# A linear-attention and feed-forward kernel on one core: q and k projected with 64 rows, two heads at once in the array's halves

## The chip, the core and the metric

The kernel runs on one core of one Trainium2 chip. A core has five engines that work side by side and meet through semaphores: TensorE (matmuls; PE in the profile, its weight loads PEld), VectorE (DVE), ScalarE (ACT), GpSimd (POOL) and SyncE (SP), which here issues nearly all the transfers between the chip's memory and the core's. Matmuls read the on-chip memory SBUF and write PSUM, which has eight banks of 512 float32 numbers on each of 128 partitions. The metric is the device time of one execution in microseconds (us).

## The reference, cut to what matters

Eight batches and eight heads, 576 tokens each, a head dimension of 64 and 128 random features; then a feed-forward block over all 4608 tokens, 512 wide with 2048 inside.

```python
def phi(x):                                    # x is q or k, times 64 ** -0.25
    proj = np.einsum('bhsd,md->bhsm', x, omega)
    sq = np.sum(x * x, axis=-1, keepdims=True) / 2.0
    h = proj - sq
    h = h - np.max(h, axis=-1, keepdims=True)
    return np.exp(h) / np.sqrt(m)
q_p, k_p = phi(q_s), phi(k_s)
kv = np.einsum('bhsm,bhsd->bhmd', k_p, v)
z = np.sum(k_p, axis=2)
num = np.einsum('bhsm,bhmd->bhsd', q_p, kv)
den = np.einsum('bhsm,bhm->bhs', q_p, z)[..., None] + 1e-06
x = num / den                                  # then, over all heads of a token:
h = x @ w_in
sp = np.maximum(h, 0.0) + np.log1p(np.exp(-np.abs(h)))
out = (h * erf(sp)) @ w_out
```

The same number sq is taken from all 128 features of a token, and then the largest feature is taken off.

## The kernel before

**Work items.** Attention goes by pairs of heads: 8 batches of 4 pairs, 32 pairs with 1152 tokens (9 chunks of 128) each. The feed-forward block goes by batch, in two halves of the 2048 inner features; its matmuls have 288 moving columns and run on operands that are split into a high and a low part (tiles xh and xl, gh and gl, and weights w with both), three matmuls for each product. Its first products are h (and hS and hA, in a form with seven products instead of eight from the fourth batch on), its second ones o.

**A pair's attention.** `load` brings q and k, transposed: 64 dimensions on the partitions, 1152 tokens along them (tiles uq and uk, into rows 0 to 63 for q and 64 to 127 for k), and v. A `square` step writes the squares of these numbers into the other 64 rows of the same tile, on GpSimd in two pieces or on ScalarE in one. `project` then runs, per chunk of 128 tokens, one float32 matmul with all 128 rows: the chunk is the stationary operand, and the moving one (wq or wk) holds the scaled omega in the rows of the numbers and the constant -0.5/8 in the rows of the squares, so that the matmul gives proj - sq at once. Three chunks share a PSUM bank (ppq or ppk), and a projection uses three banks, one after the other. VectorE takes the negated maximum of the bank's three chunks (mxq or mxk), and ScalarE the exponentials with it as the bias (fq or fk). Each bank goes through these three steps for itself. Then `key_values` multiplies fk with v (kvp), `turn` transposes fq (pt, copied to qh and ql), and `attend` forms numerator and denominator (nd), which ScalarE and VectorE divide into xs, the feed-forward block's input.

**Weights.** They come as float64 bits (st) and are rebuilt in wt by a step on GpSimd or ScalarE and three on VectorE, split into w by steps on ScalarE, GpSimd or VectorE, and stored (wdw); later uses fetch the split form.

**What sets the order.** `build` names all operations with their operands, costs and due times, and `Plan.order` places them with a list scheduler: each engine takes, among the operations that are ready and for which buffers are free, the one that is due first. The table COST gives TensorE's costs, SLOTS the number of buffers of each kind, and CAPS how many PSUM banks each stream may hold (4 for attention, 5 in the first batch). An operation may have several engines to choose from. The result is a fixed order on each engine; at run time an engine waits where an operand or a buffer isn't ready. The first batch's four pairs run ahead of all feed-forward work; from then on the pairs of the next batch lie between the matmuls of the current one. Transfers of weights are planned up to 40 us before their use.

Every instruction is recorded through one helper, so the profile shows line 742 for nearly all of them (748 in the changed file); they are told apart by their tiles. A float32 matmul of the program shows as two MATMUL records in the profile.

Of the kernel before, what the change touches and what calls it, by code (L numbers as in the profile page):

```python
# [19 lines left out]
P = 128  # L20
B, H, S, D = 8, 8, 576, 64
NP = H // 2
S2 = 2 * S
NC = S2 // P
MID = NC // 2
D1 = D + 1
DM, DF = 512, 2048
T = 288
# [32 lines left out]
SLOTS = dict(w=8, u=3, f=2, mx=3, v=2, qh=1, ql=1, kh=1, kl=1, rc=2, xs=4, xh=2, xl=2, u2=2,  # L61
             hs=4, gs=2, gh=6, gl=6, os=4, ps=8)
CAPS = dict(st=2, wt=2, cv=2, att=4, moe1=3, moe2=2)

# [250 lines left out]
SQN = 4  # L315
SQG = -1e9
SQA = 4.0
# [4 lines left out]
def build(emit):  # L322

    pl = Plan()
# [113 lines left out]
    def early(n):  # L438
        return 5 if n < NP else None

    def load(n, qk):
        a = pairs[n]

        u = a["u" + qk] = pl.tile("hs", f"u{qk}{a['nm']}", [P, S2], F32, "u0") if 0 < n < NP else \
            pl.tile("u", f"u{qk}{a['nm']}", [P, S2])
        parts = 3 if n == 0 else 1
        for i in range(parts):
            keys = [("x", c) for c in range(3)] if parts == 1 else [("x", i)]
            pl.op("load" + qk, [("S", 0.1, 1e9)], lambda e, i=i: E.x_load(u, qk, a, i, parts),
                  writes=[(u, k) for k in keys], size=D * S2 * 4 // parts)  # L450
# [4 lines left out]
        for i in range(parts):  # L455
            keys = range(3) if parts == 1 else [i]
            f = 1.0 / parts
            pl.op("sq" + qk, [("A", 1.17 * f + .1, -1e9)] if n == 0 else
                  [("G", 2.2, SQG if n < SQN else -1e9), ("A", 1.2, -1e9 if n < SQN else SQA)],
                  lambda e, i=i: E.square(e, u, qk, i, parts),  # L460
                  reads=[(u, ("x", c)) for c in keys], writes=[(u, ("s", c)) for c in keys])

    def project(n, qk, t0):
        a = pairs[n]
        u = a["u" + qk]
        f = a["f" + qk] = pl.tile("gs", f"f{qk}{a['nm']}", [P, NC, P], F32, "f0") \
            if 0 < n < NP and qk == "q" else pl.tile("f", f"f{qk}{a['nm']}", [P, NC, P])
        mx = pl.tile("mx", f"mx{qk}{a['nm']}", [P, NC])
        for i in range(3):
            pp = pl.tile("ps", f"pp{qk}{a['nm']}_{i}", [P, 512], F32, "att", early(n))  # L470
            pl.op("proj" + qk, [("T", 3 * COST["proj"], -1e9)], lambda e, i=i, pp=pp: E.project(pp, u, qk, i),
                  reads=[(u, ("x", i)), (u, ("s", i))], writes=[(pp, 0)],
                  plan=pair_time(n, t0 + 0.05 * i))
            pl.op("max" + qk, [("V", 0.56, -1e9)], lambda e, i=i, pp=pp: E.maximum(mx, pp, i),
                  reads=[(pp, 0)], writes=[(mx, i)])
            pl.op("exp" + qk, [("A", 1.1, -1e9)], lambda e, i=i, pp=pp: E.exponential(f, mx, pp, i),
                  reads=[(pp, 0), (mx, i)], writes=[(f, i)], set="exp")

    def key_values(n, t0):
        a = pairs[n]  # L480
        f, v = a["fk"], a["v"]
        kvp = a["kvp"] = pl.tile("ps", "kvp" + a["nm"], [P, 512], F32, "att", early(n))
        for j in range(2):
            pl.op("kv", [("T", (5 - j) * COST["kv"], -1e9)], lambda e, j=j: E.key_values(kvp, f, v, j),
                  reads=[(f, i) for i in range(3)] + [(v, 0)], writes=[(kvp, 0)],
                  plan=pair_time(n, t0 + 0.08 * j))
        whole = n < WHOLE
        kh = a["kh"] = pl.tile("kh", "kh" + a["nm"], [P, 2, P], F32 if whole else F32R)
        kl = a["kl"] = kh if whole else pl.tile("kl", "kl" + a["nm"], [P, 2, P], F32R)
        pl.op("kvhigh", [("V", 0.6, -1e9), ("A", 0.7, -1e9)], lambda e: E.kv_high(e, kh, kvp),  # L490
              reads=[(kvp, 0)], writes=[(kh, 0)])
        if not whole:
            pl.op("kvrest", [("V", 0.6, -1e9)], lambda e: E.kv_rest(kl, kvp, kh),
                  reads=[(kvp, 0), (kh, 0)], writes=[(kl, 0)])

    def turn(n, t0):
        a = pairs[n]
        whole = n < WHOLE
        lent = ("gh", "qh0", 2) if n < NP else ("qh", "qh", None)
        qh = a["qh"] = pl.tile(lent[0], "qh" + a["nm"], [P, S2], F32 if whole else F32R, *lent[1:])  # L500
        ql = a["ql"] = qh if whole else pl.tile("ql", "ql" + a["nm"], [P, S2], F32R)
        for i in range(3):
            pt = pl.tile("ps", f"pt{a['nm']}_{i}", [P, 512], F32, "att", early(n))
            pl.op("turn", [("T", 3 * COST["tr"], -1e9)], lambda e, i=i, pt=pt: E.turn(pt, a["fq"], i),
                  reads=[(a["fq"], i)], writes=[(pt, 0)], plan=pair_time(n, t0 + 0.05 * i))
# [216 lines left out]


@with_exitstack
def tile_attention_moe(ctx: ExitStack, tc: tile.TileContext, qT, kT, vP, omT, w1, w2, out):
# [32 lines left out]
    dve.memset(eps, 1e-6 * P)  # L758

    wq = const.tile([P, P], F32, name="wq")  # L760
    wk = const.tile([P, P], F32, name="wk")
# [5 lines left out]
    half_sq = -0.5 / math.sqrt(D)  # L767
    dve.memset(wk[0:D], half_sq)
    dve.memset(wq[D:P], half_sq)
    dve.tensor_scalar_mul(wk[D:P], om[D:P], scale)  # L770
    dve.tensor_scalar_mul(wq[0:D], om[0:D], scale)

    def copy(e, dst, src):
        if e == "A":
# [9 lines left out]
    def halves(e, n):  # L784

        return (slice(0, n // 2), slice(n // 2, n)) if e == "G" else (slice(0, n),)
# [5 lines left out]
    class Emit:  # L792
# [40 lines left out]
        def fetch(self, dst, src):  # L833
            sp.dma_start(dst, src)

        def x_load(self, u, qk, a, i, parts):
            src = (kT if qk == "k" else qT)[a["b"], a["p"]]
            r = slice(D, P) if qk == "k" else slice(0, D)
            c = slice(i * S2 // parts, (i + 1) * S2 // parts)
            sp.dma_start(u.ap[r, c], src[:, c])  # L840

        def v_load(self, v, a):
            sp.dma_start(v.ap, vP[a["b"], a["p"]])

        def square(self, e, u, qk, i, parts):
            c = slice(i * S2 // parts, (i + 1) * S2 // parts)
            src, dst = (slice(D, P), slice(0, D)) if qk == "k" else (slice(0, D), slice(D, P))
            if e == "G":
                for h in halves(e, S2 // parts):
                    pool.tensor_mul(u.ap[dst, c][:, h], u.ap[src, c][:, h], u.ap[src, c][:, h])  # L850
            else:
                act.activation(u.ap[dst, c], u.ap[src, c], AF.Square)


        def project(self, pp, u, qk, i):
            for c in range(3):
                pe.matmul(pp.ap[:, c * P:(c + 1) * P], lhsT=u.ap[:, (3 * i + c) * P:(3 * i + c + 1) * P],
                          rhs=wq if qk == "q" else wk, start=True, stop=True)

        def maximum(self, mx, pp, i):  # L860
            dve.tensor_reduce(mx.ap[:, 3 * i:3 * i + 3],
                              pp.ap[:, :3 * P].rearrange("p (c m) -> p c m", c=3), axis=AX.X,
                              op=ALU.max, negate=True)

        def exponential(self, f, mx, pp, i):
            for c in range(3):
                act.activation(f.ap[:, 3 * i + c, :], pp.ap[:, c * P:(c + 1) * P], AF.Exp,
                               bias=mx.ap[:, 3 * i + c:3 * i + c + 1])

        def key_values(self, kvp, f, v, j):  # L870

# [164 lines left out]
```

## Time and profile before

| | |
|---|---|
| Time, median of 3 runs | 1103.33 us (1102.34 to 1104.43) |
| Span of the profiled execution | 1101.4 us, on the one core |
| ppk and ppq MATMUL records | 576 each, mean 279 and 275 ns |
| kvp MATMUL records | 576, of which 512 with 65 columns, mean 269 ns |
| o MATMUL records | 3072, mean 298 and 295 ns |
| maxima mxk and mxq on VectorE | 96 each, mean 556 and 557 ns |
| exponentials fk and fq on ScalarE | 288 each, mean 371 ns |
| moved by transfers | 231.27 MB, mean 210 GB/s |

The times are those of unprofiled runs. The span is that of one profiled execution, from its first to its last instruction; a small time around it is not in it. A row of a group gives count, busy time, mean duration, and the idle time of its engine just before it with the releaser. Durations of matmuls are modelled and overlap: the profile's next start, not the duration, tells what one costs in a stream.

### The profile page before, as it was taken

The numbers are of one execution on the slowest core, as the hardware profiler recorded it, in microseconds if no ns is written. First come the engines' busy times: TensorE is split into PE (matmuls) and PEld (weight loads), VectorE is DVE, ScalarE is ACT, GpSimd is POOL, SyncE is SP. The second block draws the span as 40 slices with busy tenths as digits, with TensorE's granted clock in tenths as the row PEclk, the third lists the DMA queues.
The fourth block names the chain that finished last, engine by engine and source line by source line (L and its number), as shares of the span: only waits on it lengthen the run. The fifth ranks groups of instructions, "written<-read, shape, count | busy, mean of one in ns | idle before, by whom it ended". The sixth has DMA issues, their size and how long they took to land.

```text
span 1101.4 us, 21514 instructions
## 1 busy us (share of the span) xinstructions
PE 1074.1 (98%) x8272; PEld 1063.9 (97%) x8272; DVE 715.1 (65%) x1257; ACT 709.0 (64%) x1354; POOL 435.1 (40%) x353
## 2 busy tenths in 40 slices
PE   7798899999999999999999999999999999999998
PEld 6698899999999999999999999999999999999998
DVE  5967789876377575955757566675656766464541
ACT  7777769776578766756647667476566764654440
POOL 6535336210075294822436343343334413252300
PEclk9899899999999999999999999999999999999999
DMA  8546568675557666666666777657765666567771
GB/s 241 174 132 205 173 231 279 198 257 162 171 176 251 205 204 242 190 215 226 216 211 207 225 216 222 211 181 247 232 225 185 214 216 208 193 226 278 254 241 58
DMA packets 70117, 231.27 MB, mean 210 GB/s; under 512 B 8288, under 2 KB 8672, under 8 KB 70016
## 3 DMA queue, kind: packets, MB, share of 16 engines
q1 hardware_dynamic: 69952, 229.84, 63.9%
q8 instruction: 66, 1.08, 0.4%
q14 instruction: 35, 0.29, 0.1%
q0 software_dynamic: 64, 0.07, 0.0%
HBM read 195.26 MB, written 34.60 MB: 209 GB/s over the span
## 4 chain that ended last, share of the span: by engine, by line
PE 91%; DVE 4%; ACT 1%; issue 1%; DMA 1%; SPq 1%; POOL 0%; DVEq 0%
PE o L742 36%; PE h L742 13%; PE hS L742 11%; PE hA L742 8%; PE ppq L742 5%; PE kvp L742 5%; PE ppk L742 5%; PE nd L742 5%; PE pt L742 2%; DVE wt L742 1%; DMA uk<-kT 1%; SPq L742 1%; DVE qh L742 0%; DVE hs L742 0%; DVE mxk L742 0%
## 5 line engine op out<-in xcount | busy, mean ns | idle before, releaser
L742 PE MATMUL o<-gh,w 128*128 128x288 f32 x2048 | 444.8, 298 | 7.8 <-POOL w L742 7.4
L742 PEld LDWEIGHTS o<-gh,w 128*128 128x128 f32 x2048 | 338.9, 188 | 9.0 <-POOL w L742 8.0
L742 PE MATMUL o<-gl,w 128*128 128x288 f32 x1024 | 301.9, 295 | 0.0
L742 PEld LDWEIGHTS o<-gl,w 128*128 128x128 f32 x1024 | 192.7, 188 | 0.2
L742 PE MATMUL h<-xh,w 128*128 128x288 f32 x768 | 178.8, 305 | 0.9 <-ACT hs L742 0.9
L742 PE MATMUL hS<-xh,wS 128*128 128x288 f32 x640 | 165.7, 302 | 1.1 <-issue 1.1
L742 ACT ACTIVATE fk<-ppk,mxk 128x128 f32<-128x128 f32 x288 | 83.3, 371 | 78.0 <-DVE mxk L742 77.6
L742 PEld LDWEIGHTS h<-xh,w 128*128 128x128 f32 x768 | 131.2, 191 | 1.6 <-ACT hs L742 1.3
L742 PE MATMUL hA<-xh,w 128*128 128x288 f32 x480 | 122.1, 299 | 0.0
L742 ACT ACT_TABLE_LOAD x92 | 118.0, 1283 | 2.4 <-PEq L1027 0.7
L742 PEld LDWEIGHTS hS<-xh,wS 128*128 128x128 f32 x640 | 114.8, 189 | 1.3 <-issue 1.3
L742 PE MATMUL h<-xl,w 128*128 128x288 f32 x384 | 113.9, 297 | 0.0
L742 ACT ACTIVATE fq<-ppq,mxq 128x128 f32<-128x128 f32 x288 | 83.2, 371 | 40.0 <-DVE mxq L742 39.5
L742 POOL TENSOR_TENSOR gl<-hs,gh 128x576 fp32r<-128x576 f32 x50 | 86.5, 1753 | 42.2 <-ACT gh L742 25.8
L742 POOL TENSOR_TENSOR uq<-uq 64x576 f32<-64x576 f32 x40 | 46.4, 1178 | 139.6 <-DMA uq<-qT 98.1
L742 POOL TENSOR_TENSOR hs<-gs,hs 128x576 f32<-128x576 f32 x40 | 65.1, 1649 | 85.8 <-ACT gs L742 66.0
L742 DVE TENSOR_REDUCE mxk<-ppk 128x3 f32<-128x384 f32 x96 | 52.8, 556 | 68.9 <-PE ppk L742 67.8
L742 PE MATMUL hS<-xl,wS 128*128 128x288 f32 x320 | 94.5, 295 | 0.0
L742 POOL TENSOR_TENSOR uk<-uk 64x576 f32<-64x576 f32 x44 | 53.5, 1234 | 93.1 <-DMA uk<-kT 91.6
L742 ACT ACTIVATE gh<-hs 128x1152 fp32r<-128x1152 f32 x49 | 56.4, 1164 | 48.1 <-DVE hs L742 19.4
L742 PEld LDWEIGHTS hA<-xh,w 128*128 128x128 f32 x480 | 85.9, 189 | 0.0
L742 PE MATMUL ppk<-wk,uk 128*128 128x128 f32 x576 | 79.2, 279 | 4.4 <-DVE wk L742 4.1
(94 smaller groups left out, 2124.4 us busy)
## 6 DMA issues: line engine op xcount, KB each, us to landing
w<-wdw SPq DMA_DIRECT2D x184, 512.0 KB, 4.3
wS<-wdcS SPq DMA_DIRECT2D x80, 512.0 KB, 4.0
st<-w SPq DMA_DIRECT2D x32, 512.0 KB, 5.2
wdw<-w SPq DMA_DIRECT2D x32, 512.0 KB, 3.9
v<-vP SPq DMA_DIRECT2D x32, 325.0 KB, 3.5
w<-wdw SPq DMA_DIRECT2D x40, 256.0 KB, 3.7
out<-os SPq DMA_DIRECT2D x32, 288.0 KB, 4.0
uk<-kT SPq DMA_DIRECT2D x31, 288.0 KB, 4.2
```

The costliest lines, as they stand in the source:

```text
L742: return tc.keep_in_program_order(method(*args, **kwargs))
```

## The change

**Projection.** The tiles uq and uk now hold both heads of a pair at once: the first head's 64 dimensions in rows 0 to 63, the second's in rows 64 to 127, with 512 tokens of each side by side (4 chunks), and a last chunk with the remaining 64 tokens of both heads, zeros elsewhere. A matmul of a chunk of one head has 64 rows. Four chunks of the first head go to one PSUM bank, four of the second to another, in turns, and the last chunk takes one matmul with 128 rows and a third bank. Both moving operands are the scaled omega, in both halves of the rows. These operations are planned as two, the eight half matmuls and the last one.

**Sums of squares.** A second copy of q and k comes with tokens on the partitions (tiles yq and yk, 128 x 9 x 64). GpSimd or ScalarE squares it in place, and VectorE sums over the 64 dimensions (tiles sq and sk). After the maxima of all three banks a step on VectorE adds the half sum to the negated maximum and takes it off again, in two instructions over 9 numbers per partition: the first gives the maximum of proj - sq, the second the bias that belongs to proj alone. All exponentials of a projection come after that.

**Buffers and order.** The u tiles of the first batch no longer borrow other buffers, there are 2 buffers for y and 4 for the sums, and the planner knows the new operations with their costs.

```diff
-COST = dict(mm=0.132, proj=0.222, tr=0.109, kv=0.222, table=1.3)
+COST = dict(mm=0.132, proj=0.222, half=0.112, tr=0.109, kv=0.222, table=1.3)
...
+        u = a["u" + qk] = pl.tile("u", f"u{qk}{a['nm']}", [P, WIDE + P])
+        pl.op("load" + qk, [("S", 0.1, 1e9)], lambda e: E.x_load(u, qk, a), writes=[(u, 0)],
+              size=P * (WIDE + P) * 4)
+        y = pl.tile("y", f"y{qk}{a['nm']}", [P, NC, D])
+        pl.op("loadn", [("S", 0.1, 1e9)], lambda e: E.n_load(y, qk, a), writes=[(y, 0)],
+              size=P * NC * D * 4)
...
+        pl.op("square", [("A", 0.68, -1e9)] if n == 0 else [("G", 1.3, -1e9), ("A", 0.68, SQA)],
+              lambda e: E.square(e, y), reads=[(y, 0)], writes=[(y, 0)])
+        pl.op("sumsq", [("V", 0.72, -1e9)], lambda e: E.sum_squares(sq, y),
+              reads=[(y, 0)], writes=[(sq, 0)])
...
-        for i in range(3):
-            pp = pl.tile("ps", f"pp{qk}{a['nm']}_{i}", [P, 512], F32, "att", early(n))
-            pl.op("proj" + qk, [("T", 3 * COST["proj"], -1e9)], lambda e, i=i, pp=pp: E.project(pp, u, qk, i),
-                  reads=[(u, ("x", i)), (u, ("s", i))], writes=[(pp, 0)],
-                  plan=pair_time(n, t0 + 0.05 * i))
-            pl.op("max" + qk, [("V", 0.56, -1e9)], lambda e, i=i, pp=pp: E.maximum(mx, pp, i),
-                  reads=[(pp, 0)], writes=[(mx, i)])
...
+        banks = [pl.tile("ps", f"pp{qk}{a['nm']}_{i}", [P, 512], F32, "att", early(n)) for i in range(3)]
+        pl.op("proj" + qk, [("T", 8 * COST["half"], -1e9)], lambda e: E.project(banks[0], banks[2], u, qk),
+              reads=[(u, 0)], writes=[(banks[0], 0), (banks[2], 0)], plan=pair_time(n, t0))
+        pl.op("projm" + qk, [("T", COST["proj"], -1e9)], lambda e: E.project_mid(banks[1], u, qk),
+              reads=[(u, 0)], writes=[(banks[1], 0)], plan=pair_time(n, t0 + 0.05))
...
+        pl.op("less", [("V", 0.33, -1e9)], lambda e: E.shift(mx, sq),
+              reads=[(mx, i) for i in range(3)] + [(sq, 0)], writes=[(mx, i) for i in range(3)])
...
+        def project(self, low, high, u, qk):
+            w = wq if qk == "q" else wk
+            for c in range(4):
+                for r, b in ((slice(0, D), low), (slice(D, P), high)):
+                    pe.matmul(b.ap[:, c * P:(c + 1) * P], lhsT=u.ap[r, c * P:(c + 1) * P], rhs=w[r],
+                              start=True, stop=True)
+
+        def project_mid(self, b, u, qk):
+            pe.matmul(b.ap[:, :P], lhsT=u.ap[:, WIDE:], rhs=wq if qk == "q" else wk, start=True, stop=True)
...
+        def shift(self, mx, sq):
+
+            for x in (half_sq, -half_sq):
+                dve.scalar_tensor_tensor(mx.ap, sq.ap, x, mx.ap, op0=ALU.mult, op1=ALU.add)
```

The order on TensorE, for the k projection of the first pair of the fifth batch. Before, two of its three banks with the feed-forward matmuls between them (x3 is three program matmuls in a row):

```order
L742 MATMUL ppk_0_1_5127<-wk,uk_0_4458 128x128 x3
L742 MATMUL o_0_1_1_5082<-gh_0_2_4630,w_0_1_1_82_4957 128x288
L742 MATMUL o_0_1_1_5082<-gl_0_2_4710,w_0_1_1_82_4957 128x288
L742 MATMUL o_0_1_1_5082<-gh_0_2_4630,w_0_1_1_82_4957 128x288
L742 MATMUL o_0_1_1_5082<-gh_0_3_4698,w_0_1_1_82_4957 128x288
L742 MATMUL o_0_1_1_5082<-gl_0_3_4750,w_0_1_1_82_4957 128x288
L742 MATMUL o_0_1_1_5082<-gh_0_3_4698,w_0_1_1_82_4957 128x288
L742 MATMUL h_1_3_5146<-xh_0_3606,w_1_6_83_4983 128x288
L742 MATMUL h_1_3_5146<-xl_0_3619,w_1_6_83_4983 128x288
L742 MATMUL h_1_3_5146<-xh_0_3606,w_1_6_83_4983 128x288
L742 MATMUL ppk_0_2_5153<-wk,uk_0_4458 128x128 x3
```

The same projection in the changed kernel; ppk_0_0 takes the first head's chunks, ppk_0_2 the second's, ppk_0_1 the last chunk:

```order
L748 MATMUL h_1_3_5314<-xh_0_3791,w_1_6_83_5101 128x288
L748 MATMUL ppk_0_0_5365<-wq,uk_0_4666 128x128
L748 MATMUL ppk_0_2_5366<-wq,uk_0_4666 128x128
L748 MATMUL ppk_0_0_5365<-wq,uk_0_4666 128x128
L748 MATMUL ppk_0_2_5366<-wq,uk_0_4666 128x128
L748 MATMUL ppk_0_0_5365<-wq,uk_0_4666 128x128
L748 MATMUL ppk_0_2_5366<-wq,uk_0_4666 128x128
L748 MATMUL ppk_0_0_5365<-wq,uk_0_4666 128x128
L748 MATMUL ppk_0_2_5366<-wq,uk_0_4666 128x128
L748 MATMUL ppk_0_1_5377<-wq,uk_0_4666 128x128
L748 MATMUL pt_3_0_5379<-ident,fq_3_5318 128x128 x3
```

The half matmuls of a projection now stand in one block, and between block and last chunk there may be other work.

On VectorE, the maxima of the same projection, before:

```order
L742 TENSOR_REDUCE mxk_0_5119<-ppk_0_0_5103 128x3
L742 TENSOR_TENSOR S_3_5124<-R_3_5092 128x256
L742 COPY os_1_5140<-o_0_1_0_5066 128x288
L742 TENSOR_REDUCE mxk_0_5119<-ppk_0_1_5127 128x3
L742 TENSOR_TENSOR S_3_5124<-R_3_5092,S_3_5124 128x256
L742 TENSOR_REDUCE mxk_0_5119<-ppk_0_2_5153 128x3
L742 CAST qh_3_5176<-pt_3_0_5157 128x384
```

And in the changed kernel, where the sum of squares sk_0_4539 was taken 71 rows earlier:

```order
L748 TENSOR_TENSOR cS_2_1_5375<-S_2_5227,cS_2_1_5375 128x2x256
L748 TENSOR_REDUCE mxk_0_5392<-ppk_0_0_5365 128x4
L748 TENSOR_REDUCE mxk_0_5392<-ppk_0_2_5366 128x4
L748 TENSOR_TENSOR ql_3_5416<-pt_3_0_5379,qh_3_5390 128x384
L748 TENSOR_REDUCE mxk_0_5392<-ppk_0_1_5377 128x1
L748 SCALAR_TENSOR_TENSOR mxk_0_5392<-sk_0_4539,mxk_0_5392 128x9 x2
L748 TENSOR_TENSOR S_3_5397<-R_3_5255,S_3_5397 128x256
```

The maxima have moved together, and the two shifting instructions stand between the last of them and the exponentials.

More of the change, by code (lines that the diff above doesn't have):

```diff
@@ L25 @@
 MID = NC // 2
+WIDE = MID * P
+CHUNKS = (range(0, MID), range(MID, MID + 1), range(MID + 1, NC))
 D1 = D + 1
@@ L454, in load @@
                   size=P * (NC + 1) * D1 * 4)
[L455 to L461, printed above, removed]
+        sq = a["s" + qk] = pl.tile("sq", f"s{qk}{a['nm']}", [P, NC])
+        pl.op("square", [("A", 0.68, -1e9)] if n == 0 else [("G", 1.3, -1e9), ("A", 0.68, SQA)],
+              lambda e: E.square(e, y), reads=[(y, 0)], writes=[(y, 0)])
+        pl.op("sumsq", [("V", 0.72, -1e9)], lambda e: E.sum_squares(sq, y),
+              reads=[(y, 0)], writes=[(sq, 0)])
     def project(n, qk, t0):
         a = pairs[n]
-        u = a["u" + qk]
+        u, sq = a["u" + qk], a["s" + qk]
         f = a["f" + qk] = pl.tile("gs", f"f{qk}{a['nm']}", [P, NC, P], F32, "f0") \
@@ L468, in project @@
         mx = pl.tile("mx", f"mx{qk}{a['nm']}", [P, NC])
[L469 to L477 removed]
+        banks = [pl.tile("ps", f"pp{qk}{a['nm']}_{i}", [P, 512], F32, "att", early(n)) for i in range(3)]
[3 more added lines that the diff above has]
+              reads=[(u, 0)], writes=[(banks[1], 0)], plan=pair_time(n, t0 + 0.05))
+        for i in (0, 2, 1):
+            c = CHUNKS[i]
+            pl.op("max" + qk, [("V", 0.15 + 0.135 * len(c), -1e9)],
+                  lambda e, i=i, c=c: E.maximum(mx, banks[i], c),
+                  reads=[(banks[i], 0)], writes=[(mx, i)])
+        pl.op("less", [("V", 0.33, -1e9)], lambda e: E.shift(mx, sq),
+              reads=[(mx, i) for i in range(3)] + [(sq, 0)], writes=[(mx, i) for i in range(3)])
+        for i in (0, 2, 1):
+            c = CHUNKS[i]
+            pl.op("exp" + qk, [("A", 0.371 * len(c), -1e9)],
+                  lambda e, i=i, c=c: E.exponential(f, mx, banks[i], c),
+                  reads=[(banks[i], 0), (mx, i)], writes=[(f, k) for k in c], set="exp")
     def key_values(n, t0):
@@ L484, in key_values @@
             pl.op("kv", [("T", (5 - j) * COST["kv"], -1e9)], lambda e, j=j: E.key_values(kvp, f, v, j),
-                  reads=[(f, i) for i in range(3)] + [(v, 0)], writes=[(kvp, 0)],
+                  reads=[(f, i) for i in range(NC)] + [(v, 0)], writes=[(kvp, 0)],
                   plan=pair_time(n, t0 + 0.08 * j))
@@ L504, in turn @@
             pl.op("turn", [("T", 3 * COST["tr"], -1e9)], lambda e, i=i, pt=pt: E.turn(pt, a["fq"], i),
-                  reads=[(a["fq"], i)], writes=[(pt, 0)], plan=pair_time(n, t0 + 0.05 * i))
+                  reads=[(a["fq"], 3 * i + k) for k in range(3)], writes=[(pt, 0)], plan=pair_time(n, t0 + 0.05 * i))
             pl.op("turnhigh", [("A", 0.5, -1e9), ("V", 0.5, -1e9)],
@@ L724, in tile_attention_moe @@
 @with_exitstack
-def tile_attention_moe(ctx: ExitStack, tc: tile.TileContext, qT, kT, vP, omT, w1, w2, out):
+def tile_attention_moe(ctx: ExitStack, tc: tile.TileContext, qT, kT, qN, kN, vP, omT, w1, w2, out):
     nc = tc.nc
@@ L834, in fetch, with x_load, n_load @@
             sp.dma_start(dst, src)
[L836 to L840, printed above, removed]
+        def x_load(self, u, qk, a):
+            sp.dma_start(u.ap, (kT if qk == "k" else qT)[a["b"], a["p"]])
+        def n_load(self, y, qk, a):
+            sp.dma_start(y.ap.rearrange("p c d -> p (c d)"), (kN if qk == "k" else qN)[a["b"], a["p"]])
@@ L842, in v_load, with square @@
         def v_load(self, v, a):
             sp.dma_start(v.ap, vP[a["b"], a["p"]])
-        def square(self, e, u, qk, i, parts):
-            c = slice(i * S2 // parts, (i + 1) * S2 // parts)
-            src, dst = (slice(D, P), slice(0, D)) if qk == "k" else (slice(0, D), slice(D, P))
+        def square(self, e, y):
             if e == "G":
-                for h in halves(e, S2 // parts):
-                    pool.tensor_mul(u.ap[dst, c][:, h], u.ap[src, c][:, h], u.ap[src, c][:, h])
-            else:
-                act.activation(u.ap[dst, c], u.ap[src, c], AF.Square)
@@ L855, in project @@
[L855 to L868, printed above, removed]
+                for h in (slice(0, 4), slice(4, NC)):
+                    pool.tensor_mul(y.ap[:, h], y.ap[:, h], y.ap[:, h])
+            else:
+                act.activation(y.ap, y.ap, AF.Square)
+        def sum_squares(self, sq, y):
+            dve.tensor_reduce(sq.ap, y.ap, axis=AX.X, op=ALU.add)
@@ L870, in key_values, with exponential @@
+        def shift(self, mx, sq):
+            for x in (half_sq, -half_sq):
+                dve.scalar_tensor_tensor(mx.ap, sq.ap, x, mx.ap, op0=ALU.mult, op1=ALU.add)
+        def exponential(self, f, mx, b, c):
+            for i, k in enumerate(c):
+                act.activation(f.ap[:, k, :], b.ap[:, i * P:(i + 1) * P], AF.Exp,
+                               bias=mx.ap[:, k:k + 1])
         def key_values(self, kvp, f, v, j):
```

32 lines of the change are left out of this document (17 added, 15 removed).

## The prediction

> **What bounds the kernel now.** I read the head of the page and its chain of work first, then the busy time in four stretches, then TensorE's own waits, then single matmuls.
>
> ```profile
> span 1101.4 us, 21514 instructions
> PE 1074.1 (98%) x8272; PEld 1063.9 (97%) x8272; DVE 715.1 (65%) x1257; ACT 709.0 (64%) x1354; POOL 435.1 (40%) x353
> PE 91%; DVE 4%; ACT 1%; issue 1%; DMA 1%; SPq 1%; POOL 0%; DVEq 0%
> ```
>
> TensorE is busy 98% of the span and is 91% of the chain that ended last. Matmul ends are modelled, so that share alone proves little; the stretches (busy us and count for each engine) and the waits bear it out.
>
> ```profile
> core 0: us, PE busy (x) PEld busy (x) DVE busy (x) ACT busy (x) POOL busy (x), PEclk, DMA share, GB/s
> 0.00:55.00 55.00, 42.81 (x297) 37.78 (x298) 41.17 (x79) 42.19 (x122) 31.64 (x37) 0.94 0.70 208
> 55.00:106.00 51.00, 51.00 (x376) 49.30 (x376) 37.04 (x58) 37.64 (x80) 22.80 (x24) 0.97 0.52 172
> 106.00:115.00 9.00, 1.56 (x5) 0.79 (x4) 8.38 (x8) 8.94 (x10) 7.01 (x6) 0.70 0.47 172
> 115.00:1102.00 987.00, 978.74 (x7598) 976.07 (x7597) 628.47 (x1115) 620.25 (x1144) 373.65 (x288) 0.99 0.65 212
> ```
>
> There are two regimes. From 115 us to the end TensorE is busy 978.7 of 987 us at a granted clock of 0.99. Before that it stands still, above all from 106 to 115 us. Its waits over the whole run:
>
> ```profile
> PE o L742 <- POOL w L742: 7.4, 2, 6.9
> PE nd L742 <- DVE qh L742: 6.8, 6, 2.5
> PE ppk L742 <- DVE wk L742: 4.1, 1, 4.1
> POOL w L742 <- DVE wt L742: 13.5, 5, 5.9
> ```
>
> The first three rows are TensorE's longest; the 6.9 us is the hole at 106 us. The last row, of the waits between 55 and 120 us, says who is late there: GpSimd makes the split weights w and itself waits for VectorE's wt steps. So early time hangs on VectorE and the weight conversion, and after 115 us each microsecond taken from TensorE's stream should come off the span.
>
> What a projection costs, from the timeline (start, duration, engine, group):
>
> ```profile
> 302.76 1.44 PEld L742 LDWEIGHTS ppq<-wq,uq 128*128 128x128 f32 x12
> 304.12 0.19 PEld L742 LDWEIGHTS h<-xh,w 128*128 128x128 f32 x1
> 310.26 0.99 PEld L742 LDWEIGHTS kvp<-v,fk 128*128 128x128 f32 x8
> 311.18 0.19 PEld L742 LDWEIGHTS o<-gh,w 128*128 128x128 f32 x1
> L742 PE MATMUL ppk<-wk,uk 128*128 128x128 f32 x576 | 79.2, 279 | 4.4 <-DVE wk L742 4.1 <-DVE xs L742 0.4
> ```
>
> Twelve projection loads take 304.12 - 302.76 = 1.36 us, 113 ns each. Eight loads of kvp, with only 65 moving columns, take 0.92 us, 115 ns each. A float32 step thus costs one weight load of 113 ns, whatever its columns. The program has 32 x 9 matmuls for ppk and the trace 576, so each float32 matmul is two steps, and a projection is 18 steps, 18 x 0.113 = 2.03 us.
>
> How many lie in each regime: these are the rows of the same stretches for ppk, then for ppq.
>
> ```profile
> 115.00:1102.00 987.00, 61.78 (x450) 57.21 (x450) 41.63 (x75) 65.53 (x225) 0.99 0.65 212
> 115.00:1102.00 987.00, 62.00 (x468) 58.24 (x468) 43.49 (x78) 67.75 (x234) 0.99 0.65 212
> ```
>
> 450 + 468 = 918 steps, 51 projections, lie in the saturated stretch; the other 13 of 64 lie before it.
>
> **TensorE's part of the change.** The steps stay 18: 16 with 64 rows, 2 with 128. If the lower half's step runs while the upper half's does, 16 steps fill 8 slots. The order is low, high, low, high, and each matmul is two steps in a row on its own half; steps that start in order can only pair from the second one on, which makes 9 slots. I take 9: the saving is 16 - 9 = 7 slots x 0.113 = 0.79 us a projection, 51 x 0.79 = 40.3 us. With 8 slots it is 0.90 and 46.1 us. With no overlap it is nothing. No row of before has a 64-row matmul (all read 128*128), so these are the ends.
>
> The Trainium skill, TensorE: Matmul & The Clock Gate, section "Measured speedup vs the span model", gives 3.07x for four 32-row tiles of 512 columns, 77% of ideal; the same share for two halves would make a pair group 1.81 / 1.54 = 1.18 us, a saving of 32 us and about 1075 us. No run yet shows it for float32.
>
> **VectorE's part.** These are the nearest rows:
>
> ```profile
> L742 DVE TENSOR_REDUCE mxk<-ppk 128x3 f32<-128x384 f32 x96 | 52.8, 556 | 68.9 <-PE ppk L742 67.8
> L742 DVE COPY qh<-pt 128x384 f32<-128x384 f32 x16 | 8.6, 553 | 2.4 <-PE pt L742 2.3
> L742 DVE COPY os<-o 128x288 f32<-128x288 f32 x34 | 15.5, 457 | 49.2 <-PE o L742 49.2
> L742 DVE TENSOR_SCALAR wk<-om 64x128 f32<-64x128 f32 x1 | 0.2, 224 | 2.5 <-DMA om<-omT 2.5
> L742 DVE MEMSET eps<- 128x1 f32 x1 | 0.1, 59 | 0.8 <-PEq L1027 0.8
> ```
>
> The two copies differ by 96 elements and 96 ns, so an element costs 1 ns over some 0.17 us. The maxima become 0.69 + 0.69 + 0.30 = 1.68 us against 3 x 0.556 = 1.67: no change. New are the sum over 576 elements, 0.75 us, and two tiny steps of 9 elements, between 0.06 and 0.22 us each, say 0.17: together 1.09 us a projection, 70 us in all. In the saturated stretch that is 51 x 1.09 = 56 us on top of 628.5, 684 in about 947 us or 72%: hidden beside TensorE. Before 115 us it is 13 x 1.09 = 14.2 us on top of 86.6 (the sum of three rows above): 100.8 of 115, where VectorE is what is late. The price there lies between -10.3 us (TensorE's own 13 x 0.79, if that sets the pace) and +14.2 us (all of it on the path). The hole at 106 us waits for VectorE and GpSimd and for nothing of TensorE, so I take the loss to be the likelier sign, but the planner can hand conversions to other engines: +4 us.
>
> **Squares, loads, waits.** The squares get lighter:
>
> ```profile
> L742 POOL TENSOR_TENSOR uk<-uk 64x576 f32<-64x576 f32 x44 | 53.5, 1234 | 93.1 <-DMA uk<-kT 91.6 <-PE kvp L742 0.9 <-PE pt L742 0.3
> L742 ACT ACTIVATE uk<-uk 64x1152 f32<-64x1152 f32 x9 | 10.5, 1167 | 7.0 <-DMA uk<-kT 4.4 <-DMA w<-wdw 2.5
> L742 ACT ACTIVATE fk<-ppk,mxk 128x128 f32<-128x128 f32 x288 | 83.3, 371 | 78.0 <-DVE mxk L742 77.6
> ```
>
> GpSimd's two pieces of 1.23 us shrink to 256 and 320 elements of 576, about 1.3 us in all; ScalarE's 1.17 us halves. Both engines have slack, so: nothing. The exponentials (18 a pair at 371 ns) stay. The loads of a projection grow from 64 x 1152 x 4 = 294,912 bytes (the 288.0 KB of the last row here) to 128 x 640 x 4 and 128 x 576 x 4, 327,680 bytes more:
>
> ```profile
> DMA  8546568675557666666666777657765666567771
> GB/s 241 174 132 205 173 231 279 198 257 162 171 176 251 205 204 242 190 215 226 216 211 207 225 216 222 211 181 247 232 225 185 214 216 208 193 226 278 254 241 58
> uk<-kT SPq DMA_DIRECT2D x31, 288.0 KB, 4.2
> ```
>
> In the saturated stretch 51 x 0.328 = 16.7 MB in 947 us add 18 GB/s to 212 x 987 / 947 = 221: 239, below the 279 of the busiest slice. SyncE issues two loads where it issued one; the second can be stuck behind the two y buffers, and weight fetches behind it, but these are planned up to 40 us ahead against the 4.2 us that such a load takes to land: nothing. The first projection starts when one whole load has landed instead of a third of it, at most 1 us later, within the bounds of the early stretch.
>
> The new wait: every exponential of a projection now follows all maxima, the sum and the shift, so the first one stands about 3 us behind the first matmul (1.02 + 0.23 + 1.68) instead of 6 x 0.113 + 0.56 = 1.23, and all three PSUM banks are held that long. Behind it queue kvp and the transposes, but TensorE has h and o matmuls in between.
>
> **Sum.** The profiled execution has a span of 1101.4 us; the median of the three times, 1103.33, lies 1.9 us above, which I leave as it is. 1103.3 - 40.3 + 4 = **1067 us**. By the ends alone it is 1103.3 - 46.1 - 10.3 = 1047 up to 1103.3 - 40.3 + 14.2 = 1077.
>
> **Rivals.**
>
> *Entering and leaving the halved array costs time.* The program has 51 such groups in the saturated stretch, 102 changes. If the array must empty first, each exposes a matmul's tail:
>
> ```profile
> L742 PE MATMUL o<-gh,w 128*128 128x288 f32 x2048 | 444.8, 298 | 7.8 <-POOL w L742 7.4 <-DVE w L742 0.2 <-DMA w<-wdw 0.2
> 302.63 0.29 PE L742 MATMUL h<-xl,w 128*128 128x288 f32 x1
> 302.76 0.30 PE L742 MATMUL h<-xh,w 128*128 128x288 f32 x1
> ```
>
> A duration of 0.298 against 0.13 between starts leaves 0.166 us: 102 x 0.166 = 16.9, so 1084 us. Nothing in the trace speaks for it but that it has no change of shape of this kind. The Trainium skill, TensorEngine Tiling (Array Packing), section "Key Properties", says that a change of tiling mode drains the engine; by that rule this case would hold. Chance 0.18.
>
> *The halves run one after the other: slower.* If weight loads go in single file, 16 half loads cost what 16 full ones do. The kvp rows speak for this: 113 to 115 ns is the load's own pace. Nothing is saved, VectorE's early 4 us remain, and the time is 1107 us. It decides the sign once a half step averages over 113 - 4000 / (51 x 16) = 108 ns. It is also the case that the change doesn't do what it says. Chance 0.11.
>
> *The longer chain shows on TensorE.* The page has six stalls of nd on qh, 1.13 us each. If each of the 25 pairs of the saturated stretch had one, that is 28 us: 1095. Against it: hardly any stall of that sort falls after 115 us now. Chance 0.07.
>
> **How the numbers follow.** My case, halves that overlap and VectorE hidden, has a chance of 0.62, at 1067; the draining array 0.18, the single file 0.11, the longer chain 0.07; 0.02 is left for gains and losses that cancel. The range runs from 1047 (all good ends) to 1088 (the draining array with another 4 us early); outside lie the single file, the longer chain and the remnant, 0.20. What a measurement here can tell from no change is about 0.2%. Faster by more than that: 0.62 + 0.18 + 0.07 = 0.87; slower 0.11; the same 0.02.
>
> **What would show it.** Right: weight loads of ppk 0_0 and 0_2 in pairs, a group of 16 steps in 0.9 to 1.05 us, TensorE still free of waits after 115 us, VectorE near 72%. Draining: holes of 0.1 us or more at the group's ends. Single file: 1.8 us a group. Early stretch: the hole before the first o grows by some 4 us. I am wrong most simply if a group takes over 1.2 us, or if TensorE waits for fq, fk or qh in every pair.

## The result, and the profile after

The changed kernel takes 1130.00 us (median of three, 1128.61 to 1131.61) against 1103.33: ratio 1.0243, 95% interval 1.0228 to 1.0258. It is slower by 26.7 us where 36 less were forecast, 63 us above the forecast of 1067. These are the head of its page and its chain:

```profile
span 1126.8 us, 21814 instructions
PE 1067.3 (95%) x8272; PEld 1031.2 (92%) x8272; DVE 783.7 (70%) x1443; ACT 697.4 (62%) x1354; POOL 411.4 (37%) x361
PE 81%; DVE 10%; ACT 4%; issue 2%; POOL 1%; DMA 1%; ACTq 0%; DVEq 0%; POOLq 0%
```

TensorE is still the longest, but VectorE and ScalarE have come onto the chain: 14% where they had 5%. The same four stretches as before (the last one ends 25 us later):

```profile
0.00:55.00 55.00, 39.69 (x241) 33.74 (x243) 37.13 (x77) 33.18 (x97) 21.66 (x33) 0.88 0.74 250
55.00:106.00 51.00, 45.56 (x324) 41.60 (x322) 36.74 (x74) 35.13 (x85) 16.10 (x20) 0.87 0.55 176
106.00:115.00 9.00, 7.14 (x63) 6.75 (x60) 7.91 (x15) 8.59 (x25) 5.50 (x7) 1.00 0.83 294
115.00:1127.00 1012.00, 974.88 (x7658) 949.15 (x7656) 701.95 (x1280) 620.50 (x1149) 368.14 (x303) 0.99 0.66 224
```

After 115 us TensorE is idle 37 us where it was idle 8, and the stretch, with 7658 matmul records instead of 7598, is 25 us longer although its projections are shorter. In the trace of before no wait there came to more than 1.1 us. Now there are two of 2.3 us on ScalarE's hs and three of up to 1.8 us on GpSimd's w between 115 and 200 us, and these are the largest sums of TensorE's waits from 200 to 1127 us (us in total, times, longest):

```profile
PE pt L748 <- DVE u L748: 6.3, 3, 2.4
PE nd L748 <- DVE ql L748: 2.6, 3, 1.7
PE hA L748 <- DVE hs L748: 2.3, 2, 1.6
```

VectorE's evacuations, the reads that empty a PSUM bank, are late: after 115 us the profile lists some 33 us of waits of TensorE and puts 22 of them down to VectorE; in the trace of before it is 1.6 of some 4. VectorE is busy 702 of 1012 us, 69%: it isn't full, it is late at certain moments.

A wait can cost more than its own length. From 576.1 to 579.5 us, right behind a wait of 2.4 us, the granted clock is 0.50, and matmuls with 288 columns start 240 ns apart where at the full clock it is 132. After 115 us and without the last microseconds, the clock records show 20.5 us at half clock in the changed kernel and 8.3 in the kernel before. By these figures the 12.2 us more lose about 12.2 x (1 - 132 / 240) = 5.5 us, which is an estimate: not every long wait is followed by a slow stretch, and no run tests the clock by itself.

**The packing itself works.** The half matmuls of one projection in the timeline:

```profile
568.86 0.29 PE L748 MATMUL hA<-xh,w 128*128 128x288 f32 x1
569.08 1.16 PE L748 MATMUL ppk<-wq,uk 64*128 64x128 f32 x16
570.17 0.40 PE L748 MATMUL hS<-xh,wS 128*128 128x288 f32 x1
570.41 0.29 PE L748 MATMUL hS<-xl,wS 128*128 128x288 f32 x1
```

Sixteen steps lie within 1.16 us; one after the other they would take 16 x 0.113 = 1.81. The gaps at the edges have grown: 0.22 us from the hA matmul to the first half where a stream has 0.13. From the hA matmul to the second hS matmul it is 1.55 us, which is also the median of the groups after 115 us. In the kernel before, the same distance around twelve full steps starts with the h matmul at 302.76 of the prediction's rows and goes on with these:

```profile
302.89 1.50 PE L742 MATMUL ppq<-wq,uq 128*128 128x128 f32 x12
304.15 0.38 PE L742 MATMUL h<-xh,w 128*128 128x288 f32 x1
304.36 0.29 PE L742 MATMUL h<-xl,w 128*128 128x288 f32 x1
```

It is 304.36 - 302.76 = 1.60 us, so sixteen full steps would take 1.60 + 4 x 0.113 = 2.05. A group saves 0.50 us, and 51 groups 26 us. That the stretch is 25 us longer even so leaves 51 us to explain: 29 are TensorE's additional idle time, some 8 the 60 records more, at 0.13 each, and about 5 the clock. The other 9 don't show as idle time and stay open.

**VectorE's new work.** Groups by form:

```profile
L748 DVE SCALAR_TENSOR_TENSOR mxk<-sk,mxk 128x9 f32<-128x9 f32 x64 | 24.8, 388 | 2.0
L748 DVE SCALAR_TENSOR_TENSOR mxq<-sq,mxq 128x9 f32<-128x9 f32 x64 | 15.5, 242 | 2.2
L748 DVE TENSOR_REDUCE sq<-yq 128x9 f32<-128x576 f32 x32 | 23.9, 747 | 0.8 <-POOL yq L748 0.6
L748 DVE TENSOR_REDUCE mxk<-ppk 128x4 f32<-128x512 f32 x64 | 41.6, 684 | 23.0 <-PE ppk L748 22.9
```

Sum and maximum are what was estimated (0.75 and 0.69). The shift, two instructions over nine numbers, is not: 388 and 242 ns on average for work that I put at 170. One moment shows what it does (VectorE, GpSimd and TensorE, in order of time):

```profile
573.32 2.78 POOL L748 TENSOR_TENSOR gl<-hs,gh 128x576 fp32r<-128x576 f32 x2
573.47 2.65 DVE L748 SCALAR_TENSOR_TENSOR mxk<-sk,mxk 128x9 f32<-128x9 f32 x2
576.04 0.44 DVE L748 TENSOR_TENSOR u<-hS,hs 128x288 f32<-128x288 f32 x1
576.54 0.90 PE L748 MATMUL pt<-ident,fq 128*128 128x128 f32 x3 [2.39 <-DVE u L748]
```

GpSimd has just begun two pieces of 1.4 us each. Each of the two shift instructions ends with one of them, together 2.65 us. Behind them on VectorE stands the reading of a finished hS bank (into u), and TensorE waits 2.39 us for it before it can transpose. Of the 128 shift instructions of the trace, 89 start when no GpSimd tensor instruction runs or begins within 150 ns, and last 171 ns on average; the other 39 last 645, and where they last over 250 they end 26 ns (median) behind the end of GpSimd's piece. The sums read the same memory and last 746 ns with or without a running piece.

### The profile page after: what moved, and what is told of

Its sections match the earlier page's. It is cut to its first block, busy times and chain, and to the rows that moved or that the text cites. A ratio compares the mean times of both kernels' runs of the same rounds, so it can differ in the third digit from the quotient of the medians.

```text
span 1126.8 us, 21814 instructions
## 1 busy us (share of the span) xinstructions
PE 1067.3 (95%) x8272; PEld 1031.2 (92%) x8272; DVE 783.7 (70%) x1443; ACT 697.4 (62%) x1354; POOL 411.4 (37%) x361
## 4 chain that ended last, share of the span: by engine, by line
PE 81%; DVE 10%; ACT 4%; issue 2%; POOL 1%; DMA 1%; ACTq 0%; DVEq 0%; POOLq 0%
PE o L748 34%; PE h L748 12%; PE hS L748 10%; PE hA L748 8%; PE kvp L748 5%; PE ppk L748 3%; PE nd L748 3%; PE ppq L748 3%; PE pt L748 2%; DVE mxk L748 2%; DVE hs L748 2%; DVE wt L748 1%; ACT gs L748 1%; ACT rc L748 1%; ACT L748 1%
## 5 line engine op out<-in xcount | busy, mean ns | idle before, releaser
L748 PE MATMUL o<-gh,w 128*128 128x288 f32 x2048 | 439.8, 297 | 5.8 <-POOL w L748 3.7
L748 PE MATMUL hS<-xh,wS 128*128 128x288 f32 x640 | 160.1, 303 | 4.0 <-ACT fq L748 1.7
L748 POOL TENSOR_TENSOR hs<-gs,hs 128x576 f32<-128x576 f32 x44 | 71.9, 1655 | 210.2 <-ACT gs L748 210.2
L748 POOL TENSOR_TENSOR gl<-hs,gh 128x576 fp32r<-128x576 f32 x56 | 97.3, 1761 | 37.5 <-ACT gh L748 19.0
L748 ACT ACTIVATE fq<-ppq,mxq 128x128 f32<-128x128 f32 x288 | 77.7, 387 | 51.7 <-DVE mxq L748 46.8
L748 DVE TENSOR_TENSOR os<-o,os 128x288 f32<-128x288 f32 x64 | 29.2, 456 | 81.2 <-PE o L748 80.7
L748 ACT ACTIVATE fk<-ppk,mxk 128x128 f32<-128x128 f32 x288 | 78.6, 386 | 11.3 <-DVE mxk L748 11.0
L748 ACT ACTIVATE rc<-nd,eps 64x288 f32<-64x288 f32 x128 | 60.0, 493 | 40.2 <-PE nd L748 24.0
L748 ACT ACTIVATE gs<-hs 128x1152 f32<-128x1152 f32 x64 | 72.1, 1160 | 10.7 <-DVE hs L748 10.3
L748 PE MATMUL kvp<-v,fk 128*128 128x65 f32 (+1 forms) x576 | 73.7, 282 | 4.7 <-ACT fk L748 3.4
```

The lines of the kernel that those rows point to most:

```text
L748: return tc.keep_in_program_order(method(*args, **kwargs))
```

## The experiments

Theory 1 was that the shift, which waits for GpSimd, holds up VectorE and through it TensorE. The rivals were VectorE's load as such, the early loads, and the joint wait for three banks. Medians below stand beside the kernel before on the same chip, 1103.24 for the first four runs, 1102.92 and 1102.69 for the next two sets, 1102.30 for the last; the sets ran on different chips, so a difference of about 1 us between runs of different sets tells nothing.

**Without the shift, same order.**

```diff
         def shift(self, mx, sq):
-            for x in (half_sq, -half_sq):
-                dve.scalar_tensor_tensor(mx.ap, sq.ap, x, mx.ap, op0=ALU.mult, op1=ALU.add)
+            return
```

> The changed kernel with the same order on every engine, but the two instructions that add the half sum of squares to the maxima and take it off again are left out (128 in all); the sums themselves are still formed. Theory 1, the shift waits for GpSimd and holds up VectorE, and VectorE's later evacuations hold up TensorE: these 128 instructions take 40 us on VectorE, where 128 x 0.17 = 22 us would do, and the stalls of TensorE after 200 us that follow them go: 1085 to 1100 us. Rival 2, VectorE's load and the three banks held together set the time, and the shift is only a small part of the load: 1120 to 1128 us.

Measured: 1112.07 us, ratio to before 1.0077 (1.0051 to 1.0102). That is 18 us less, more than the rival's 2 to 10 and less than the 30 to 45 of theory 1: both sizes miss. 128 instructions, 40.3 us of a VectorE that is idle nearly a third of the time, cost 18 us of the whole. Leaving them out also shortens the chain from the maxima to the exponentials; the run with the shift on GpSimd, below, bears on which of the two counts.

**Without the second copy and the sums, same order.** This edit is made on top of the first one.

```diff
         def n_load(self, y, qk, a):
-            sp.dma_start(y.ap.rearrange("p c d -> p (c d)"), (kN if qk == "k" else qN)[a["b"], a["p"]])
+            return
         def square(self, e, y):
...
+            return
         def sum_squares(self, sq, y):
-            dve.tensor_reduce(sq.ap, y.ap, axis=AX.X, op=ALU.add)
+            return
```

> As the run without the shift, and the second copy of q and k is neither loaded nor squared nor summed (left out: all sums of squares); order otherwise the same. Theory 1: only VectorE's 48 us of sums and the loads go in addition, which lie beside TensorE's work; 5 to 12 us below the run without the shift, most of it in the first 120 us. Rival 2 (VectorE's load): 20 us or more below it. Rival 3 (the early loads are what hurts): the first matmul starts near 5 us instead of 7, and the stretch up to 200 us gets shorter by 15 us or more against the run without the shift.

Measured: 1101.08 us, ratio 0.9982 (0.9959 to 1.0005), another 11 us, within theory 1's 5 to 12. Some 6 of them lie before 115 us, where 684 matmul records have started against 637 in the run without the shift. TensorE's first matmul starts at 6.8 us, so the early loads are not what delays it. With none of the new work left in the program, this order only reaches the time of before.

**The same work, planned anew.** All operations for the sums of squares are taken out ahead of the planner, and each exponential needs its own bank's maximum alone:

```diff
-        pl.op("loadn", [("S", 0.1, 1e9)], lambda e: E.n_load(y, qk, a), writes=[(y, 0)],
-              size=P * NC * D * 4)
...
-        pl.op("square", [("A", 0.68, -1e9)] if n == 0 else [("G", 1.3, -1e9), ("A", 0.68, SQA)],
-              lambda e: E.square(e, y), reads=[(y, 0)], writes=[(y, 0)])
-        pl.op("sumsq", [("V", 0.72, -1e9)], lambda e: E.sum_squares(sq, y),
-              reads=[(y, 0)], writes=[(sq, 0)])
...
-        pl.op("less", [("V", 0.33, -1e9)], lambda e: E.shift(mx, sq),
-              reads=[(mx, i) for i in range(3)] + [(sq, 0)], writes=[(mx, i) for i in range(3)])
```

> The changed kernel with all operations for the sums of squares taken out ahead of the planner (left out: all sums of squares, the second loads, the shift), so that the order is planned anew and each bank's exponentials follow its own maximum. If the packing itself works: 51 projections x (0.90 - 0.3) = 30 us below the kernel before in the saturated stretch and something early: 1060 to 1075 us. If holding two banks for one step is what stalls TensorE: 1080 us or more.

Measured: 1074.66 us, ratio 0.9744 (0.9729 to 0.9759). The instructions are the same kinds on TensorE as in the run before it, in another order, and 26 us go. Its page and its last stretch:

```profile
span 1072.4 us, 21317 instructions
PE 1041.0 (97%) x8272; PEld 1010.9 (94%) x8272; DVE 696.1 (65%) x1260; ACT 670.0 (62%) x1306; POOL 365.8 (34%) x291
115.00:1073.00 958.00, 943.52 (x7540) 924.92 (x7538) 612.77 (x1118) 584.92 (x1090) 327.57 (x247) 1.00 0.65 219
```

TensorE's idle time after 115 us is 14 us here, against 37. The 29 us below the kernel before nearly add up: 51 x 0.50 = 26 from the halves and some 8 from 58 records fewer after 115 us (7540 against 7598), less 6 for the idle time, 14 against 8. Leaving the sums out changes the result by rounding alone: the half sum is one number per token, and the maximum over the features takes it off again.

**Full rows in the changed order.** Each half matmul takes 128 rows, with zeros for the other head in two new moving operands (wlow and whigh, made once at the start):

```diff
...
-                for r, b in ((slice(0, D), low), (slice(D, P), high)):
-                    pe.matmul(b.ap[:, c * P:(c + 1) * P], lhsT=u.ap[r, c * P:(c + 1) * P], rhs=w[r],
+                for w, b in ((wlow, low), (whigh, high)):
+                    pe.matmul(b.ap[:, c * P:(c + 1) * P], lhsT=u.ap[:, c * P:(c + 1) * P], rhs=w,
                               start=True, stop=True)
```

> The changed kernel in the same order, but each of the eight half matmuls takes all 128 rows, with zeros in the other head's rows of the moving operand: same result, no overlap of halves, no change of shape. TensorE's work grows by 64 x 0.90 = 57 us, the changes of shape (about 0.3 us a projection, 19 us) go. If TensorE's stream sets the time now: 1160 to 1172 us. If the stalls that are there take up the longer projections: 1135 to 1150 us. If the halves did not really overlap: 1110 to 1130 us.

Measured: 1154.97 us, ratio 1.0472 (1.0457 to 1.0488), 25 us above the changed kernel: between the two cases. In this order the overlap is worth 25 us, where 64 x 0.50 = 32 us of TensorE's stream hang on it.

**64 rows and no pairs.** The kernel before without its squares, planned anew; each matmul takes the 64 rows of the numbers.

```diff
...
+                r = slice(0, D) if qk == "q" else slice(D, P)
-                pe.matmul(pp.ap[:, c * P:(c + 1) * P], lhsT=u.ap[:, (3 * i + c) * P:(3 * i + c + 1) * P],
-                          rhs=wq if qk == "q" else wk, start=True, stop=True)
+                pe.matmul(pp.ap[:, c * P:(c + 1) * P], lhsT=u.ap[r, (3 * i + c) * P:(3 * i + c + 1) * P],
+                          rhs=(wq if qk == "q" else wk)[r], start=True, stop=True)
```

> The kernel before without its squares (left out: all sums of squares); each projection matmul takes the 64 rows of the numbers alone, in one half of the array, never two at once. If a 64-row step costs what a 128-row one does, TensorE's stream is as long as before: 1095 to 1104 us, and the packing owns nearly all of the distance to 1074.66. If the squares' work on ScalarE and GpSimd was what cost: below 1085 us.

Measured: 1145.28 us, ratio 1.0385 (1.0370 to 1.0401). Neither case: 42 us slower than before with less work. Its timeline says why:

```profile
span 1143.3 us, 21310 instructions
PE 1129.9 (99%) x8272; PEld 1082.3 (95%) x8272; DVE 702.3 (61%) x1256; ACT 686.9 (60%) x1329; POOL 344.1 (30%) x271
615.39 0.29 PE L735 MATMUL hS<-xh,wS 128*128 128x288 f32 x1
615.61 0.93 PE L735 MATMUL ppk<-wk,uk 64*128 64x128 f32 x6
616.47 0.40 PE L735 MATMUL hS<-xh,wS 128*128 128x288 f32 x1
616.71 0.29 PE L735 MATMUL hS<-xl,wS 128*128 128x288 f32 x1
```

From the hS matmul ahead of six steps to the second one behind them it is 1.32 us; by the row of twelve full steps it would be 1.60 - 6 x 0.113 = 0.92. Entering and leaving cost 0.40 us together, 0.20 a change of shape. After 115 us the median for six steps between feed-forward matmuls is 1.32 here and 0.94 with full steps in the kernel before, a difference of 0.39. The trace has 287 such changes, 260 of them after 115 us: 52 us at this price, where that stretch is 42 us longer than before (1029 against 987). The other 10 are not accounted for. In the packed kernel it is the same: eight slots and no price for the change would give 2.05 - 8 x 0.113 = 1.15, the row gives 1.55, and 0.40 is the difference.

**Which part of the plan made the order worse.** Four runs ask that. First, only the joint wait, as an edit of the run planned anew:

```diff
-                  reads=[(banks[i], 0), (mx, i)], writes=[(f, k) for k in c], set="exp")
+                  reads=[(banks[i], 0)] + [(mx, k) for k in range(3)], writes=[(f, k) for k in c], set="exp")
```

> The replanned kernel without sums of squares (1074.66 us), with one thing more: in the plan every exponential of a projection waits for the maxima of all three banks, as in the changed kernel; no instruction is added (left out as there: all sums of squares). If the joint wait, which holds three banks together and puts all exponentials behind the last maximum, makes up the 26 us between the runs without sums in the old and in the new order: 1090 to 1102 us. If it was the place of the sums in the plan that made the old order worse: 1073 to 1079 us.

Measured: 1076.06 us, ratio 0.9775 (0.9735 to 0.9816). The joint wait is not it: 1.4 us is within this run's noise. Then an empty operation in the shift's place:

```diff
+        pl.op("less", [("V", 0.33, -1e9)], lambda e: None,
+              reads=[(mx, i) for i in range(3)], writes=[(mx, i) for i in range(3)])
```

> The replanned kernel without sums of squares (1074.66 us), with an empty operation in the plan where the shift stood, on VectorE with its cost of 0.33 us; it emits nothing (left out: all sums of squares). If the shift's place in the plan made the old order worse by 26 us: 1090 to 1101 us. If not: 1073 to 1080 us, as with the joint wait alone.

Measured: 1086.84 us, ratio 0.9854 (0.9830 to 0.9879): 12 us for an operation that emits nothing, short of the 15 to 26 expected of it. Next, the changed kernel planned anew without the shift but with loads, squares and sums:

```diff
-        pl.op("less", [("V", 0.33, -1e9)], lambda e: E.shift(mx, sq),
-              reads=[(mx, i) for i in range(3)] + [(sq, 0)], writes=[(mx, i) for i in range(3)])
...
-                  reads=[(banks[i], 0), (mx, i)], writes=[(f, k) for k in c], set="exp")
+                  reads=[(banks[i], 0), (mx, i), (sq, 0)], writes=[(f, k) for k in c], set="exp")
```

> The changed kernel planned anew without the shift (left out: adding the half sum and taking it off again); second copy, squares and sums stay, and an exponential waits in the plan for its own bank's maximum and for the sums. If the joint wait was the cause: 1080 to 1092 us, the run without sums plus some 10 us for the sums. If the sums in the plan were: 1100 to 1112 us.

Measured: 1089.12 us, ratio 0.9869 (0.9854 to 0.9884). That lies in the range named for the joint wait, but the run with this wait alone has ruled it out; the shift left the plan here too. The first experiment emits the same work in the full plan's order and takes 1112.07, so the order alone makes 23 us here. And the same order with loads, squares and sums emitting nothing (the edit of the second experiment):

> The order of the run with sums and without joint wait (1089.12 us), but loads, squares and sums emit nothing (left out: all sums of squares). If the sums' own work and transfers cost the 14.5 us between that run and 1074.66: 1073 to 1079 us. If it was their place in the plan: 1084 to 1090 us.

Measured: 1085.01 us, ratio 0.9831 (0.9808 to 0.9853): the sums' place in the plan costs 10 us, carrying them out only 4 more. The second experiment emits the same work in the full plan's order and takes 1101.08, 16 us more.

**How much is luck.** One number of the plan is changed, the cost of a half matmul, 0.13 for 0.112:

> The replanned kernel without sums of squares, with one number of the plan changed that has no meaning for the work: 0.13 instead of 0.112 us for a half matmul. It measures what another, equally reasonable order is worth. If orders differ by luck as much as the 26 us in question: 8 us or more away from 1074.66. If not: within 4 us.

Measured: 1079.91 us, ratio 0.9799 (0.9776 to 0.9823). A change without meaning moves the time by 5 us, between the two cases, so the 12 and the 10 above are not much more than twice what an accident of the order is worth.

**The planner told of the wait.** The complete changed kernel, with the shift on the list of operations that wait for GpSimd:

```diff
-SHARED = ("wshift", "wsign", "wtail", "wrest", "wwhole", "wsum", "xsum", "xhigh", "xrest", "gate",
+SHARED = ("wshift", "wsign", "wtail", "wrest", "wwhole", "wsum", "xsum", "xhigh", "xrest", "gate", "less",
```

> The changed kernel, complete, but the planner counts the shift among VectorE's operations that wait for a running piece of GpSimd, so the order is planned with that wait. If the mistaken cost in the plan is what hurts: 1105 to 1118 us. If the wait itself does, wherever it stands: 1122 to 1135 us.

Measured: 1120.94 us, ratio 1.0158 (1.0128 to 1.0187), 9 us less than the changed kernel and between the two cases.

**The shift on GpSimd.** The complete changed kernel, planned anew:

```diff
-        pl.op("less", [("V", 0.33, -1e9)], lambda e: E.shift(mx, sq),
+        pl.op("less", [("G", 0.5, -1e9)], lambda e: E.shift(mx, sq),
...
-            for x in (half_sq, -half_sq):
-                dve.scalar_tensor_tensor(mx.ap, sq.ap, x, mx.ap, op0=ALU.mult, op1=ALU.add)
+            pool.tensor_scalar(sq.ap, sq.ap, half_sq, 0.0, op0=ALU.mult, op1=ALU.add)
+            pool.tensor_add(mx.ap, mx.ap, sq.ap)
+            pool.tensor_sub(mx.ap, mx.ap, sq.ap)
```

> The complete changed kernel, planned with the shift on GpSimd, as three small instructions over 9 numbers (scale, add, take off) instead of two on VectorE. If the price of the shift is VectorE's wait for running pieces of GpSimd, it is gone and only the plan and the sums are left: 1095 to 1112 us. If a shift between maxima and exponentials costs the same on any engine, because the chain is longer: 1122 to 1135 us.

Measured: 1110.35 us, ratio 1.0074 (1.0057 to 1.0090). The chain is as long as in the changed kernel, and the longer way on GpSimd takes more time for itself (rows by form: 298 and 295 ns for each addition):

```profile
L748 POOL TENSOR_TENSOR mxq<-mxq,sq 128x9 f32<-128x9 f32 x64 | 19.1, 298 | 144.6 <-DVE mxq L748 141.0 <-POOL sq L748 0.2
L748 POOL TENSOR_TENSOR mxk<-mxk,sk 128x9 f32<-128x9 f32 x64 | 18.9, 295 | 88.3 <-DVE mxk L748 85.0
```

Still 20 us of the changed kernel's time are gone, about what leaving the shift out saved, and the time lies in the range for VectorE's wait, 1095 to 1112. This was planned anew, so some of it may be the order; but the case in which a shift costs the same on any engine, 1122 to 1135, is out.

**Omega first.** The run planned anew with the two small loads of omega ahead of all others on SyncE:

```diff
-    pool.dma_start(om[D:P], omT)
-    pool.dma_start(om[0:D], omT)
+    sp.dma_start(om[0:D], omT)
+    sp.dma_start(om[D:P], omT)
```

> The replanned kernel without sums of squares, in the same order, with the two loads of omega issued by SyncE ahead of all others instead of by GpSimd. There TensorE's first matmul waits 7.6 us for the scaled omega, against 4.1 in the kernel before. If the whole early chain hangs on it, the time falls by 2 to 3 us, to 1072; if other work early on is later anyway, it stays within 1 us.

Measured: 1073.99 us, ratio 0.9741 (0.9714 to 0.9768), 0.7 us less, which is no difference, although TensorE's first matmul starts at 5.2 us instead of 7.6. It and the run it comes from are the fastest of the study, some 29 us below the kernel before.

## Why the prediction was wrong, step by step

The distance from 1067 to 1130.00 is closed by the runs: 1074.66 - 1067 = 7.7 for the packing without sums (the forecast held 4 us for the sums); 1101.08 - 1074.66 = 26.4 for the order that the full plan makes; 1112.07 - 1101.08 = 11.0 for carrying out loads, squares and sums; 1130.00 - 1112.07 = 17.9 for the shift. These are steps along one path, each with the others as they stand there.

- **"The saving is 16 - 9 = 7 slots x 0.113 = 0.79 us a projection."** The mechanism was right and the size off: the halves overlap, in eight slots even, but a group saves 0.50, since the two changes of shape cost 0.40. 51 x 0.29 = 15 us are missing from the saving.
- **The draining array, given 0.18.** Its price is what the runs show, 0.20 us a change where the tail gave 0.166. The Trainium skill, TensorEngine Tiling (Array Packing), section "Key Properties", says that changing the tiling mode drains TensorE; the trace agrees in that each change has a price, 260 changes after 115 us in the unpaired run and a stretch 42 us longer, but it doesn't show the array emptying, since ends of matmuls are modelled.
- **"684 in about 947 us or 72%: hidden beside TensorE."** This is the step that failed and turned the sign. The new work on VectorE, with its loads and squares, costs 18 + 11 = 29 us in this order; without it the changed kernel takes 1101.08, level with the kernel before. A share is an average; 69% busy still leaves moments at which an evacuation stands behind other work while TensorE waits for its bank, and TensorE's idle time after 115 us went from 8 to 37 us. The stretch after 115 us was read as "TensorE sets the time", which was so only as long as the other engines kept just ahead.
- **"Two tiny steps of 9 elements, say 0.17."** The bounds, 0.06 to 0.22, came from instructions of the first 5 us with at most one input. The real price is 0.17 alone and up to 1.35 us behind a piece of GpSimd's. The code had the hint: its planner lists VectorE's operations that wait so. The Trainium skill, SBUF — State Buffer, section "SBUF: two separate sides", says that VectorE and GpSimd share a port pair, that a VectorE instruction with two inputs in SBUF and a GpSimd one that reads SBUF lock each other out of it, and that the one that starts first keeps it for its whole length. The trace agrees, with 645 against 171 ns, and the sums with one input stay at 746; no run here changes the number of inputs alone.
- **"Squares, loads: nothing."** Together with the sums on VectorE they cost 11 us in the changed order and 4 in a better one. The transfers moved 224 GB/s in the last stretch, 239 were estimated.
- **The early stretch, +4.** By 115 us TensorE has started 59 matmul records fewer than before, 48 of h, 8 of nd and 3 of o, and 60 more lie behind that mark (7658 against 7598): some 8 us at 0.13 each, twice what was forecast. The granted clock of the first two stretches, 0.88 and 0.87 against 0.94 and 0.97, goes with it. The first matmul waited for the scaled omega until 7.1 us, before until 4.1, but by the last experiment such a delay costs nothing.
- **The longer chain, given 0.07 at 1095.** Wrong as it was meant: after 115 us TensorE waits once for fq (1.7 us), once for fk (0.3), never for qh, and its three waits of nd for ql come to 2.6 us. The joint wait by itself costs 1.4 us, within the noise. An operation between maximum and exponential costs 12, through the plan.
- **The single file, the rival on the slower side.** Wrong: the halves overlap. The kernel got slower for another reason, which no rival named.
- **The order.** The prediction costed each edit in the old order and never asked what the planner's new one would be worth, 26 us, as much as the halves save. Why operations on VectorE lead it to an order that is 10 to 26 us worse stays open: the empty shift explains 12 and the empty sums 10, and one meaningless number 5.

## What to carry to other kernels

When the bound engine is 98% busy, the others keep up by a margin that their busy shares don't show; work added to them has to be priced by who queues behind it, not by their share. Small instructions want a look at what they share with a neighbour engine: two in each projection, 0.17 us each when undisturbed, cost 18 us of the run. And packing halves cost about 0.40 us for each group here, whether it had six steps or sixteen, to change the array's shape and back: 0.40 / 0.113 = 3.5 slots must be saved before a group gains anything.

## What the runs showed of the hardware that was not expected

- Going to 64-row matmuls and back costs TensorE about 0.40 us, 0.20 a change on average, even where the 64-row matmuls use one half alone.
- A 64-row float32 step takes as long as a 128-row one (112 ns between starts inside the unpaired groups), and two of them in different halves overlap almost fully.
- A two-input VectorE instruction over nine numbers lasts up to 1347 ns when GpSimd is in a piece, a sum over 576 numbers with one input isn't touched (746 ns).
- TensorE's granted clock can fall to half behind a wait of some 2 us, as from 576.1 to 579.5 us, and matmuls with 288 columns then start 240 ns apart instead of 132.
